# LSH attention followed by a gated convolution layer: part of the first batch's w_val products moved to earlier slots

## The chip, the cores and the metric

The kernel runs on one core of one Trainium2 chip. The metric is the device time of one execution in microseconds (us). The kernel before has a median of 624.18 us over three runs (622.38 to 624.53).

## The reference

Four batches of eight heads, 768 positions, head dimension 64, all in float32 (w_val, conv_w and w_out reach the kernel as float64). A hash gives each query and key a bucket of 6 bits, and a query sees only keys of its own bucket:

```
q_bits = (einsum('bhsd,dk->bhsk', q, proj) > 0)        # the same for k
mask   = q_bucket[:, :, :, None] == k_bucket[:, :, None, :]
scores = where(mask, scale * q @ k^T, -1e9)
attn   = softmax(scores);  x = (attn @ v) as (batch, 768, 512)

gate_pre = sum over k of conv_w[k] * xp[:, k:k+768, :]   # causal, 5 taps
out = (sigmoid(gate_pre) * (x @ w_val)) @ w_out
```

The products with w_val and w_out are made in three parts each (high times high, low times high, high times low), from operands that are split into a rounded high part and a remainder.

## The kernel before

The attention works on 32 units (batch, head) of six query tiles each: 192 slots, numbered k. In one turn of the main loop (L519 to L531 of the code below) stand, for different tiles, the row maximum (DVE, L272), two small DVE instructions, the normalisation (POOL, L305), the scores of tile k + 1 (PE, L266), the exponential of tile k (ACT, L290), six transposes of tile k - 3 (PE, L314) and the copy of the transposes of tile k - 4 out of PSUM (ACT, L323). In every odd slot two steps of the product with v are made (PE, L337, eight matmuls). The order on each of PE, ACT, DVE and POOL is the order in which the code issues the instructions; each engine takes its own instructions strictly in turn. DMAs stand on SP's queue.

Beside this the loop advances generators, one step at a time, and a step is where a generator yields:

- `weights`: loads a 512 KB block of float64 weight (L137), and turns it into a high and a low part on ACT (L91), DVE (L93 to L109) and POOL (L111, L113). Eight blocks, done by about slot 52.
- `ahead` (`early_bits`): hash bits of the batches 2 to 4 (units 16, 20, 24 and 28). For each it loads four tiles `hh` and four tiles `hl` (L221, 192 KB each), makes four small matmuls into the PSUM tile `m` for each half (L226), compares on DVE (L229) and stores (L231). Eight such halves, called "bit halves" below, in the slots 16, 20, 28, 32, 40, 44, 52 and 56.
- `convs` (`pair_x`): for two heads at a time (a pair; four pairs in a batch) splits x into `xh` and `xl` and adds up the convolution. The last step of a batch's fourth pair takes the sigmoid of the four gates (ACT, L372, with table loads) and starts the batch's `moe`. For the first batch this is slot 65.
- `moe`: for each half of the positions (o) and each block of 128 columns (j), `val` makes 12 matmuls of 384 columns (L399), in steps of four, and multiplies by the gate (DVE, L404); `outp` makes 12 matmuls of 512 columns (L424), in steps of four. One batch has eight `val` and six `outp`. In the two slots at the sigmoid three steps are made, else one per slot, and one in every second slot where `thin` holds (for the first batch slots 90 to 101). Before its last two `outp` a batch waits for the next batch's `moe` (`hold`).

All `val` and `outp` of the main loop, and all bits made before the first `moe`, use the single PSUM tile `m` (pool `ps_m`, one buffer): the next group can start only when the last one has been read.

Of the kernel before, what the change touches and what calls it, by code (L numbers as in the profile page):

```python
# [8 lines left out]
FP32 = mybir.dt.float32  # L9
FP32R = mybir.dt.float32r  # L10
AF = mybir.ActivationFunctionType
ALU = mybir.AluOpType
# [14 lines left out]
def kernel(  # L27
# [10 lines left out]
    nc = tc.nc  # L38
    B, H, _, S = qk.shape
    P = 128  # L40
    D = 64
    KB = S // P
    HS = S // 2
    NP = H // 2
# [306 lines left out]
    def pair_x(b, c, x, gs, xs_):  # L351
        for o in (0, HS):
            xh = xs.tile([P, HS], FP32R, name="xh")
            xl = xs.tile([P, HS], FP32R, name="xl")
            xs_[(c, o)] = (xh, xl)
            x0 = x[:, KW - 1 + o:KW - 1 + o + HS]
            nc.vector.tensor_copy(out=xh, in_=x0)  # L357
            nc.gpsimd.tensor_tensor(out=xl, in0=x0, in1=xh.bitcast(FP32), op=ALU.subtract)  # L358
        yield
        g = gp.tile([P, S], FP32, name="g")  # L360
        gs.append(g)
        for k in range(KW):
            yield
            w = cw_sb[:, c * KW + k:c * KW + k + 1]
            if k == 0:
                nc.gpsimd.tensor_scalar(out=g, in0=x[:, 0:S], scalar1=w, scalar2=1.0, op0=ALU.mult, op1=ALU.mult)  # L366
            else:
                nc.vector.scalar_tensor_tensor(out=g, in0=x[:, k:k + S], scalar=w, in1=g, op0=ALU.mult, op1=ALU.add)  # L368
        if c == NP - 1:
            yield  # L370
            for g in gs:
                nc.scalar.activation(out=g, in_=g, func=AF.Sigmoid)  # L372
            cur["gates"] = 2
            moes.append(moe(b, xs_, gs))

    def acc_tile():
        pools = accs
# [6 lines left out]
    def moe(b, xs_, g):  # L384
        hs = {}
        todo = []

        def later():
            while todo:
                todo.pop(0)()  # L390

        def val(o, j):
            acc = acc_tile()
            m = 0
            for wi, xi in ((0, 0), (1, 0), (0, 1)):
                if m:
                    yield
                for c in range(NP):
                    nc.tensor.matmul(out=acc[:, 0:HS], lhsT=wv[wi][:, c, j * P:(j + 1) * P],  # L399
                                     rhs=xs_[(c, o)][xi], start=(m == 0), stop=(m == 11))  # L400
                    m += 1
                later()
            ht = hp.tile([P, HS], FP32, name="ht", bufs=2)
            nc.vector.tensor_tensor(out=ht, in0=acc[:, 0:HS], in1=g[j][:, o:o + HS], op=ALU.mult)  # L404

            def split():
                hh = hp.tile([P, HS], FP32R, name="hh")
                nc.vector.tensor_copy(out=hh, in_=ht)  # L408
                hl = hp.tile([P, HS], FP32R, name="hl")
                nc.gpsimd.tensor_tensor(out=hl, in0=ht, in1=hh.bitcast(FP32), op=ALU.subtract)  # L410
                hs[(o, j)] = (hh, hl)
            todo.append(split)
            yield
# [43 lines left out]

    raws, stacks, vts, ss, nbs, ps, tps, sums, rcs, nms, gs, cur = {}, {}, {}, {}, {}, {}, {}, {}, {}, {}, {}, {}
    avs, convs, moes, early = [], [], [], {}
    accs = [(ps_m, "m")]  # L460

    def step(gens):

        while gens:
            try:
                return next(gens[0])
            except StopIteration:
                gens.pop(0)
# [7 lines left out]
    with tc.manual_schedule(engines=ENGINES):  # L476
# [13 lines left out]
        for k in range(N + LAG + 1):  # L490
            if 0 <= k - LAG - 1:
                keep_transposed(k - LAG - 1)
            pair = k % 2 == 0 and 0 <= k - 2 < N
            if k < N:
                maxima(k)
            if pair:
                row_sums(k - 2)
            if k < N:
                factors(k)
            if pair:  # L500
                recip(k - 2)
            if 0 <= k - 2 < N:
                normalise(k - 2)
            if k < N:
                shifts(k)
            if k + 1 < N:
                if tiles[k + 1][0] != tiles[k][0]:
                    finish(preps)
                    preps = [prep(tiles[k + 1][0] + 1)]
                scores(k + 1)  # L510
            if k < N:
                exponentials(k)
            if k >= 60 or k % 2:
                step(convs)
            for _ in range((1, 0, 2, 0, 2, 2)[k % 6]):
                step(weights[turn])
                turn = 1 - turn

            thin = k // 6 % 8 in (7, 0) and k < 186  # L519
            for _ in range(3 if cur["gates"] else (1, 0)[k % 2] if thin else 1):  # L520
                step(moes)
            cur["gates"] = max(0, cur["gates"] - 1)
            step(preps)
            if 6 <= k < 60 and k % 6 in (2, 4):
                step(ahead)
            if k % 2:
                step(avs)
                step(avs)
            if 0 <= k - LAG < N:
                transposes(k - LAG)  # L530
# [67 lines left out]
```

## Time and profile before

| | |
|---|---|
| median of three runs | 624.18 us (622.38 to 624.53) |
| profiled execution, first to last instruction | 620.8 us |
| its own time outside the span | not listed; the median lies 3.4 us above the span |
| PE busy (matmul) | 585.5 us, 94% |
| DVE, ACT, POOL busy | 437.6, 421.4, 395.6 us |
| matmuls with w_val (L399) | 384 |
| matmuls with w_out (L424) | 288 |

Slot k is told by the k-th exponential (L290): its start is taken as the slot's boundary. Slot 12 begins at 42.81 us, slot 40 at 120.54, slot 56 at 165.13, slot 60 at 175.41, slot 66 at 195.98 and slot 108 at 314.74. A busy PE counts the modelled length of overlapping matmuls, so it is not PE at its peak.

### The profile page before, as it was taken

To read this page: it belongs to the slowest core of one execution; us is meant where nothing else is said; L and a number is where in the kernel's file an instruction comes from. 1 tells how busy PE (TensorE), PEld (TensorE's weight loads), DVE (VectorE), ACT (ScalarE), POOL (GpSimd) and SP (SyncE) were. 2 spreads that over 40 slices of the span, in tenths; PEclk is the share of its full clock that TensorE was granted. 3 is DMA by queue.
4 is the path that set the end of the run, shared out by engine and by line. 5 is a ranking of instruction groups with operands and counts; after the bars stand their busy time and mean duration, and the time that the engine had idled before them with its cause. 6 is when DMAs were issued, how large, how long until landed. Compare 5 with 4: busy or idle time off the path is not lost.

```text
span 620.8 us, 10648 instructions
## 1 busy us (share of the span) xinstructions
PE 585.5 (94%) x3496; PEld 423.4 (68%) x3496; DVE 437.6 (70%) x1017; ACT 421.4 (68%) x881; POOL 395.6 (64%) x373
## 2 busy tenths in 40 slices
PE   5789898989999999999999999999999999999997
PEld 2655565555657777776767777777667877775895
DVE  5869798998975866668575867569665877665532
ACT  2777777778778666777787676777787766765400
POOL 3576868778766765578564777568764777544321
PEclk9799999999999999999999999999999999999999
DMA  6467666564532235243433234333422213200111
GB/s 227 123 197 199 200 167 208 157 175 118 133 83 68 70 79 142 72 108 82 122 82 107 61 80 126 84 115 82 108 70 78 67 42 91 69 18 1 51 52 51
DMA packets 29031, 64.64 MB, mean 104 GB/s; under 512 B 4937, under 2 KB 10057, under 8 KB 28977
## 3 DMA queue, kind: packets, MB, share of 16 engines
q1 hardware_dynamic: 28832, 63.93, 37.8%
q8 instruction: 28, 0.46, 0.3%
q14 instruction: 27, 0.21, 0.1%
q10 hardware_dynamic: 144, 0.03, 0.0%
HBM read 30.60 MB, written 7.86 MB: 62 GB/s over the span
## 4 chain that ended last, share of the span: by engine, by line
PE 66%; DVE 12%; ACT 12%; DMA 5%; issue 3%; POOL 2%; SPq 1%; ACTq 0%; POOLq 0%; DVEq 0%
PE av L337 17%; PE s L266 16%; PE tp L314 12%; PE m L424 8%; PE m L399 7%; ACT p L290 5%; DVE nm L272 4%; ACT pt L323 3%; ACT x L345 2%; DMA w<-in_w_val_dram 2%; DVE g L368 2%; PE tp L399 1%; PE tp L424 1%; PE s L424 1%; DMA bk<-bq 1%
## 5 line engine op out<-in xcount | busy, mean ns | idle before, releaser
L305 POOL TENSOR_SCALAR p<-p,ri 128x768 f32<-128x768 f32 x192 | 210.5, 1100 | 156.0 <-DVE nb L282 130.8
L272 DVE TENSOR_REDUCE nm<-s 128x1 f32<-128x768 f32 x192 | 182.5, 950 | 61.2 <-PE s L266 61.0
L290 ACT ACTIVATE p<-s,nb,gs 128x768 f32<-128x768 f32 x192 | 192.6, 1003 | 46.2 <-DVE nb L282 41.9
L323 ACT COPY pt<-tp 128x384 f32<-128x384 f32 x384 | 165.7, 485 | 75.3 <-PE tp L314 74.4
L314 PEld LDWEIGHTS tp<-ident,p 128*128 128x128 f32 x1152 | 130.3, 142 | 72.2 <-issue 43.6
L314 PE MATMUL tp<-ident,p 128*128 128x128 f32 x1152 | 164.4, 279 | 2.6 <-ACT pt L323 2.1
L337 PE MATMUL av<-pt,vt 128*64 128x384 f32 x768 | 144.9, 498 | 0.0
L266 PE MATMUL s<-ak,aq 76*128 76x384 f32 x384 | 118.1, 389 | 23.2 <-ACT p L290 19.7
L266 PE MATMUL s<-bk,bq 128*128 128x384 f32 x384 | 101.3, 345 | 0.4 <-DVE bq L252 0.4
L337 PEld LDWEIGHTS av<-pt,vt 128*64 128x64 f32 x768 | 47.0, 136 | 61.5 <-issue 61.4
L266 PEld LDWEIGHTS s<-ak,aq 76*128 76x128 f32 x384 | 59.2, 194 | 38.7 <-ACT p L290 34.6
L368 DVE SCALAR_TENSOR_TENSOR g<-x,cw_sb,g 128x768 f32<-128x768 f32 x64 | 79.4, 1241 | 2.2 <-POOL g L366 2.1
L266 PEld LDWEIGHTS s<-bk,bq 128*128 128x128 f32 x384 | 71.7, 194 | 0.8 <-issue 0.8
L173 POOL TENSOR_TENSOR bq<-r,aq 128x768 fp32r<-128x768 f32 x31 | 59.2, 1909 | 0.1
L410 POOL TENSOR_TENSOR hl<-ht,hh 128x384 fp32r<-128x384 f32 x32 | 32.3, 1009 | 39.5 <-DVE hh L408 39.5
L345 ACT COPY x<-av 64x384 f32<-64x384 f32 x64 | 30.4, 475 | 29.7 <-PE av L337 29.0
L282 DVE TENSOR_SCALAR nb<-nm,gs 128x1 f32<-128x1 f32 x192 | 40.4, 211 | 3.5
L399 PE MATMUL m<-xh,wv 128*128 128x384 f32 x200 | 42.7, 337 | 0.0
L358 POOL TENSOR_TENSOR xl<-x,xh 128x384 fp32r<-128x384 f32 x32 | 33.4, 1059 | 13.8 <-DVE xh L357 13.8
L290 ACT ACTIVATION_READ_ACCUMULATOR p<-s,nb,gs 128x1 f32 x192 | 39.0, 203 | 0.0
L404 DVE TENSOR_TENSOR ht<-m,g 128x384 f32<-128x384 f32 x25 | 13.9, 556 | 35.6 <-PE m L399 29.2
L424 PE MATMUL m<-wo,hh 128*128 128x512 f32 x144 | 38.1, 394 | 0.0
(86 smaller groups left out, 486.9 us busy)
## 6 DMA issues: line engine op xcount, KB each, us to landing
r<-in_qk_dram SPq DMA_DIRECT2D x32, 384.0 KB
vt<-in_v_dram SPq DMA_DIRECT2D x16, 384.0 KB
out_dram<-o SPq DMA_DIRECT2D x24, 256.0 KB
ak<-aq SPq DMA_DIRECT2D x31, 192.0 KB
bk<-aq SPq DMA_DIRECT2D x31, 192.0 KB
bk<-bq SPq DMA_DIRECT2D x31, 192.0 KB
bq<-aq SPq DMA_DIRECT2D x31, 192.0 KB
hh<-in_qk_dram SPq DMA_DIRECT2D x16, 192.0 KB
```

Of the source, the lines that this page charges most:

```text
L173: nc.gpsimd.tensor_tensor(out=bq, in0=r, in1=aq.bitcast(FP32), op=ALU.subtract)
L266: nc.tensor.matmul(out=s[:, hf, 0:HS], lhsT=lq[0:n, qs], rhs=rk[0:n, hf * HS:(hf + 1) * HS], start=n == M, stop=n == P)
L272: nc.vector.tensor_reduce(out=nm, in_=s[:, :, 0:HS], axis=AX.XY, op=ALU.max, negate=True)
L290: nc.scalar.activation(out=p, in_=s[:, :, 0:HS], func=AF.Exp, bias=nb, scale=gs.pop(k), accum_out=sm[:, k % 2, 0:1])
L305: nc.gpsimd.tensor_scalar(out=p, in0=p, scalar1=rcs.pop(k), scalar2=1.0, op0=ALU.mult, op1=ALU.mult)
L314: nc.tensor.transpose(out=tp[:, n * P:(n + 1) * P], in_=p[:, kb * P:(kb + 1) * P], identity=ident)
L323: nc.scalar.copy(out=pt[:, :, qo:qo + P], in_=tp[:, 0:HS].rearrange("p (a b) -> p a b", b=P))
L337: nc.tensor.matmul(out=av[s * D:(s + 1) * D, 0:HS], lhsT=vt[:, kb, hh * D:(hh + 1) * D], rhs=pt[kb // 3][:, kb % 3, :], start=(kb == 0), s ...
L345: nc.scalar.copy(out=x[hh * D:(hh + 1) * D, o:o + HS], in_=av[s * D:(s + 1) * D, 0:HS])
L368: nc.vector.scalar_tensor_tensor(out=g, in0=x[:, k:k + S], scalar=w, in1=g, op0=ALU.mult, op1=ALU.add)
L399: nc.tensor.matmul(out=acc[:, 0:HS], lhsT=wv[wi][:, c, j * P:(j + 1) * P], rhs=xs_[(c, o)][xi], start=(m == 0), stop=(m == 11))
L424: nc.tensor.matmul(out=acc, lhsT=hs[(o, j)][hi][:, tb * P:(tb + 1) * P], rhs=wo[wi][:, j, :], start=(m == 0), stop=(m == 11))
```

## The change

After the second pair of the first batch, a new generator `first_sums` is queued in `begun`. In the even slots 40 to 54 it makes, for one (o, j) each, the products of the pairs that are there: two pairs (six matmuls) for the first half of the positions, three pairs (nine matmuls) for the second. In the odd slot after it ACT copies the sum from PSUM to SBUF. Later `val` of the first batch makes only the products of the remaining pairs (six or three matmuls), adds the kept sum on DVE, and multiplies by the gate in a second DVE instruction. `thin` now holds in every slot below 108, so the first batch's `moe` makes one step in every second slot there (and three in each of the slots 65 and 66). The bits ahead are stepped in every even slot from 6 to 38, so that the eight bit halves stand in the slots 12, 14, 20, 22, 28, 30, 36 and 38.

```
+        if (b, c) == (0, 1):
+            begun.append(first_sums(xs_))
...
+    def products(acc, xs_, o, j, cs, after=None):
+
+        todo = [(wi, xi, c) for wi, xi in ((0, 0), (1, 0), (0, 1)) for c in cs]
+        for m, (wi, xi, c) in enumerate(todo):
+            if m and m % NP == 0:
+                yield
+            nc.tensor.matmul(out=acc[:, 0:HS], lhsT=wv[wi][:, c, j * P:(j + 1) * P], rhs=xs_[(c, o)][xi],
+                             start=(m == 0), stop=(m == len(todo) - 1))
+            if after and (m % NP == NP - 1 or m == len(todo) - 1):
+                after()
+
+    def first_sums(xs_):
+
+        for i, (o, j) in enumerate((o, j) for o in (0, HS) for j in range(NP)):
+            cs = (0, 1) if o == 0 else (0, 1, 2)
+            acc = ps_m.tile([P, 512], FP32, name="m")
+            for _ in products(acc, xs_, o, j, cs):
+                pass
+            yield
+            t = xs.tile([P, HS], FP32R, name=("xh", "xl")[i % 2]).bitcast(FP32)
+            nc.scalar.copy(out=t, in_=acc[:, 0:HS])
+            parts[(o, j)] = (t, cs)
+            yield
...
         def val(o, j):
             acc = acc_tile()
-            m = 0
-            for wi, xi in ((0, 0), (1, 0), (0, 1)):
-                if m:
-                    yield
-                for c in range(NP):
-                    nc.tensor.matmul(out=acc[:, 0:HS], lhsT=wv[wi][:, c, j * P:(j + 1) * P],
-                                     rhs=xs_[(c, o)][xi], start=(m == 0), stop=(m == 11))
-                    m += 1
-                later()
+            part, done = parts.pop((o, j), (None, ())) if b == 0 else (None, ())
+            yield from products(acc, xs_, o, j, [c for c in range(NP) if c not in done], later)
             ht = hp.tile([P, HS], FP32, name="ht", bufs=2)
-            nc.vector.tensor_tensor(out=ht, in0=acc[:, 0:HS], in1=g[j][:, o:o + HS], op=ALU.mult)
+            if part is None:
+                nc.vector.tensor_tensor(out=ht, in0=acc[:, 0:HS], in1=g[j][:, o:o + HS], op=ALU.mult)
+            else:
+                nc.vector.tensor_tensor(out=ht, in0=acc[:, 0:HS], in1=part, op=ALU.add)
+                nc.vector.tensor_tensor(out=ht, in0=ht, in1=g[j][:, o:o + HS], op=ALU.mult)
...
+            if 40 <= k < 60 and k % 2:
+                step(begun)
             if k >= 60 or k % 2:
                 step(convs)
...
             thin = k // 6 % 8 in (7, 0) and k < 186
+            thin = thin or k < 108
...
-            if 6 <= k < 60 and k % 6 in (2, 4):
+            if 6 <= k < 40 and k % 2 == 0:
                 step(ahead)
+            if 40 <= k < 60 and k % 2 == 0:
+                step(begun)
```

In the issue order, `m`, `s`, `tp` and `av` are PSUM tiles, `wv_120` and `wv_121` the high and low part of w_val, `w_875`, `w_994`, `w_900` and `w_1019` blocks of weight. On PE at slots 40 and 41, before:

```order
L226 MATMUL m<-hh,proj_sb 32x384 x4
L314 MATMUL tp<-ident,p 128x128 x6
L266 MATMUL s<-ak,aq 128x384 x2
L266 MATMUL s<-bk,bq 128x384 x2
L337 MATMUL av<-pt,vt 64x384 x4
```

and on PE at the same place now:

```order
L384 MATMUL m<-xh,wv_120 128x384 x2
L384 MATMUL m<-xh,wv_121 128x384 x2
L384 MATMUL m<-xl,wv_120 128x384 x2
L314 MATMUL tp<-ident,p 128x128 x6
L266 MATMUL s<-ak,aq 128x384 x2
L266 MATMUL s<-bk,bq 128x384 x2
L337 MATMUL av<-pt,vt 64x384 x4
```

The bit half has gone to an earlier slot, and six matmuls with w_val stand in its place (L384 is the new line of L399). On SP at slots 18 to 23, where the fourth block of w_val is loaded, before:

```order
L177 DMA bq<-aq 64x768
L148 DMA r<-in_qk_dram 128x768
L137 DMA w_875<-in_w_val_dram 128x1024
L231 DMA ud<-ht 128x384
L182 DMA ak<-u 12x768
L221 DMA hl<-in_qk_dram 128x384 x2
L137 DMA w_994<-in_w_out_dram 128x1024
```

and on SP at the same place now:

```order
L177 DMA bq<-aq 64x768
L148 DMA r<-in_qk_dram 128x768
L221 DMA hl<-in_qk_dram 128x384 x3
L137 DMA w_900<-in_w_val_dram 128x1024
L231 DMA ud<-ht 128x384
L182 DMA ak<-u 12x768
L231 DMA ud<-ht 128x384
L137 DMA w_1019<-in_w_out_dram 128x1024
```

Three loads of `hl` now stand ahead of the weight block. On PE at the first `outp` of the first batch, before (L424):

```order
L424 MATMUL m<-wo_122,hh 128x512 x4
L314 MATMUL tp<-ident,p 128x128 x6
L266 MATMUL s<-ak,aq 128x384 x2
L266 MATMUL s<-bk,bq 128x384 x2
L424 MATMUL m<-wo_123,hh 128x512 x4
```

and on PE at the same place now (L447):

```order
L447 MATMUL m<-wo_122,hh 128x512 x4
L314 MATMUL tp<-ident,p 128x128 x6
L266 MATMUL s<-ak,aq 128x384 x2
L266 MATMUL s<-bk,bq 128x384 x2
L337 MATMUL av<-pt,vt 64x384 x4
L314 MATMUL tp<-ident,p 128x128 x6
L266 MATMUL s<-ak,aq 128x384 x2
L266 MATMUL s<-bk,bq 128x384 x2
L447 MATMUL m<-wo_123,hh 128x512 x4
```

A step came in every slot and now comes in every second. From slot 108 to the end the order on PE, DVE and ACT is the same in both kernels.

## Rows read from the trace of the kernel before

**Rows 1.** The page, part 1: busy time of each engine, share of the span, instructions.

```profile
PE 585.5 (94%) x3496; PEld 423.4 (68%) x3496; DVE 437.6 (70%) x1017; ACT 421.4 (68%) x881; POOL 395.6 (64%) x373
```

**Rows 2.** Stretches: from:to, length; busy of PE, PEld, DVE, ACT, POOL; clock, DMA share, GB/s.

```profile
42.81:120.54 77.73, 71.14 (x459) 44.37 (x457) 68.48 (x157) 59.61 (x128) 59.03 (x55) 1.00 0.66 186
120.54:143.94 23.40, 20.55 (x134) 13.14 (x133) 22.31 (x49) 16.46 (x36) 19.82 (x17) 1.00 0.56 162
143.94:165.13 21.19, 19.19 (x122) 11.98 (x124) 19.01 (x40) 16.70 (x36) 16.07 (x16) 1.00 0.41 99
165.13:175.41 10.28, 9.42 (x64) 6.22 (x57) 7.31 (x20) 7.41 (x18) 8.35 (x10) 1.00 0.51 134
175.41:195.98 20.57, 20.09 (x131) 14.32 (x130) 14.28 (x33) 17.58 (x34) 12.20 (x12) 1.00 0.31 74
195.98:213.25 17.27, 16.36 (x101) 12.20 (x100) 14.12 (x32) 11.87 (x26) 13.14 (x13) 1.00 0.28 74
213.25:231.18 17.93, 17.86 (x110) 13.51 (x109) 12.16 (x31) 12.13 (x28) 12.97 (x13) 1.00 0.39 93
231.18:249.79 18.61, 18.61 (x110) 13.64 (x109) 11.48 (x28) 13.07 (x30) 10.86 (x12) 1.00 0.45 118
249.79:267.51 17.72, 17.65 (x110) 13.51 (x109) 11.04 (x28) 12.41 (x29) 10.42 (x11) 1.00 0.31 83
267.51:283.13 15.62, 15.30 (x98) 11.35 (x97) 12.72 (x30) 12.10 (x27) 11.52 (x12) 1.00 0.32 88
283.13:298.40 15.27, 14.34 (x90) 9.88 (x89) 10.89 (x29) 11.92 (x27) 12.12 (x12) 1.00 0.45 107
298.40:314.74 16.34, 16.10 (x98) 11.49 (x97) 11.41 (x28) 12.36 (x29) 11.20 (x11) 1.00 0.35 99
335.44:352.92 17.48, 17.40 (x110) 13.44 (x109) 12.70 (x32) 12.12 (x28) 12.02 (x12) 1.00 0.26 73
406.92:422.31 15.39, 15.31 (x98) 11.35 (x97) 11.66 (x30) 12.00 (x27) 10.91 (x12) 1.00 0.29 83
```

**Rows 3.** The same, of L290 alone: two instructions per slot.

```profile
42.81:120.54 77.73, 30.56 (x56) 1.00 0.66 186
```

**Rows 4.** Chain of waits, shares by line: 42.81 to 120.54, then 195.98 to 314.74.

```profile
by line: DVE nm L272 10.1%; DMA w<-in_w_val_dram 8.2%; issue 7.2%; DMA w<-in_w_out_dram 6.7%; DMA bk<-bq 6.5%; PE av L337 5.6%; PE s L266 5.6%; POOL bq L173 5.3%; DVE g L368 4.4%; DMA hl<-in_qk_dram 4.1%; ACT p L290 3.1%; DVE o L94 2.5%; DV
...
by line: PE av L337 24.3%; PE s L266 22.2%; PE tp L314 17.4%; PE m L424 9.4%; PE m L399 8.3%; ACT p L290 7.3%; ACT pt L323 5.3%; ACT x L345 2.6%; issue 1.9%; DVE nm L272 0.7%; DVE ht L404 0.5%; DVE nb L282 0.2%; DVE gs L278 0.1%; ACTq L290 
```

**Rows 5.** Chain of waits in the tail, where PE works without a gap: start, us, what.

```profile
577.41 2.75 PE tp L424 x12
...
582.91 2.10 PE tp L399 x12
```

**Rows 6.** DVE's waits, 42.81 to 120.54: us in total, times, longest.

```profile
DVE o L93 <- ACT o L91: 2.9, 2, 1.8
...
DVE ht L229 <- PE m L226: 1.7, 3, 1.1
```

**Rows 7.** Groups by shape: shapes, count, busy us, mean ns, idle before, releaser.

```profile
L323 ACT COPY pt<-tp 128x384 f32<-128x384 f32 x384 | 165.7, 485 | 75.3 <-PE tp L314 74.4
...
L404 DVE TENSOR_TENSOR ht<-m,g 128x384 f32<-128x384 f32 x25 | 13.9, 556 | 35.6 <-PE m L399 29.2 <-ACT g L372 3.4 <-issue 1.8
...
L229 DVE TENSOR_SCALAR ht<-m,packed 128x384 fp32r<-128x384 f32 x8 | 5.4, 676 | 4.3 <-PE m L226 4.2
```

**Rows 8.** Timeline of SP, 62 to 75 us: start, us, instruction.

```profile
66.55 0.44 SPq L137 DMA_DIRECT2D w<-in_w_val_dram  x1
...
70.98 0.98 SPq L221 DMA_DIRECT2D hl<-in_qk_dram  x2
```

**Rows 9.** Timeline of ACT: start, us, instruction, idle before it and its releaser.

```profile
72.96 0.70 ACT L91 ACTIVATE o<-w 128x512 f32<-128x512 f32 x1 [1.67 <-DMA w<-in_w_val_dram]
...
190.88 3.05 ACT L372 ACTIVATE g<-g 128x768 f32<-128x768 f32 x4
```

More of the change, by code (lines that the diff above doesn't have):

```diff
@@ L459 @@
     avs, convs, moes, early = [], [], [], {}
+    begun, parts = [], {}
     accs = [(ps_m, "m")]
```

## The prediction

> **What bounds the kernel now.** I read the page's first part, then the stretches, then the chain of waits of two of them. PE is busy for 94% of the span [rows 1], but the share is an average over two regimes, and the reader should see where they meet. From slot 66 the chain runs over PE: av, s, tp and the two products m take 82% of it, DVE about 1% (second line of [rows 4]). From slot 12 to 39 the chain mixes DVE (nm and the weights' conversion), loads of weights and POOL, and PE has no large share (first line of [rows 4]); DVE is busy for 68.48 of 77.73 us there, and for 22.31 of 23.40 us in slots 40 to 47 [rows 2]. So matmuls taken out of the slots from 66 on are worth time, and a DVE instruction put into the slots before 40 costs time.
>
> What a slot costs when PE alone sets it: the stretch at 335.44 us has six slots with one step of four 384-column matmuls each, and takes 17.48 us with PE busy for 17.40 [rows 2]. A matmul of 384 columns takes 2.10 / 12 = 0.175 us without a gap, one of 512 columns 2.75 / 12 = 0.229 us [rows 5]. That leaves (17.48 - 24 x 0.175) / 6 = 2.21 us of PE per slot for s, tp and av. The same from a thin stretch with three steps (406.92): (15.39 - 2.10) / 6 = 2.21.
>
> **The change, stretch by stretch.** The order from slot 108 on is the same, so the 306 us from 314.74 on stay. Up to slot 11 nothing moves. Between them are five terms.
>
> *Slots 12 to 39* (28 slots, by the 56 instructions of L290 [rows 3]). Four of the eight bit halves come in from slots 40 to 56: four DVE compares of 0.676 us, 2.7 us, and each waits for its own matmuls, 4.2 / 8 = 0.53 us on average [rows 7], 2.1 us more. DVE takes its instructions in turn, and behind each compare stands the next row maximum, on which exponential, scores and so the slot depend. That is 4.8 us if nothing covers it. Twice (slots 14 and 38) the bit half stands right behind bits of the next four units in the one PSUM buffer, and PE must wait for DVE to read; I count that inside the next item's spread. The loads move too: three hl loads now go out just ahead of a weight block on SP's queue. That block goes out at 66.55 us and ACT already waits 1.67 us for it, at 72.96 [rows 8, 9]. ACT takes its instructions in turn, so its exponentials stand behind this wait. Issue of three loads is 3 x 0.49 = 1.5 us [rows 8], and their 0.59 MB at the stretch's 186 GB/s [rows 2] another 3.2 us: at most 4.7 us. But the slots before have become later themselves by a bit half or two (1.2 us each), and the compares of slots 20 and 22 lie under the same wait, so I take 0.5 us net. Term: +5.3 us. Ends: 0 (DVE's 9.25 us of idle time in the stretch, of which 2.9 us is this kind of weight wait [rows 6], would hide all of it; a gain has no source, as instructions are only added) and 4.8 + 4.7 = +9.5.
>
> The Trainium skill (DMA: Bandwidth & Descriptors, section Queues, rings and completion order) says that on each DMA engine descriptors are consumed in ring order. By that rule the block waits for all of the three loads, and the upper end holds; the block took 6.4 us from issue to ACT's start here, which neither confirms nor excludes it. It is the second rival below.
>
> *Slots 40 to 55.* PE gets 4 x 6 + 4 x 9 = 60 matmuls, 60 x 0.175 = 10.5 us. The stretch takes 23.40 + 21.19 = 44.59 us now, set by DVE. Three bit halves leave it, and DVE's 41.32 us fall to 39.3. PE needs 16 x 2.21 + 10.5 = 45.9 us, so the bound passes from DVE to PE, and the stretch becomes longer, not shorter. With both engines over 80% busy the nearest row is the stretch at 195.98 us, where PE is busy for 16.36 of 17.27 us with DVE at 82%: some 2 to 5% of gaps. I take 47.0 us: +2.4 us. Ends: +1.3 (no gap) and +6.9 (nothing of the matmuls is hidden: 10.5 less three bit halves of 1.2). The eight ACT copies, 0.485 us each by the copy of the same shape from PSUM [rows 7], lie beside ACT's idle time (33.2 busy of 44.6 us) and each follows an exponential whose scores PE made just before the sum, so it finds it ready; the next sum wants the buffer a slot later. If that cover went, 8 x 0.485 = 3.9 us, within the upper end.
>
> *Slots 56 to 59.* One bit half leaves: 0.68 + 0.53 = 1.2 us at most. DVE has more idle time here (7.31 of 10.28 us busy), so I take -1.0; ends -1.2 and 0.
>
> *Slots 60 to 65, the sigmoid.* Slots 65 and 66 make 18 matmuls in place of 24, but the four sigmoids and two table loads hold ACT until slot 66 begins at 195.98 [rows 9], and PE's work lies beside that. The added DVE adds lie there too. Term 0; ends -1.0 and +1.7 (three adds of 0.556 us [rows 7] that are not hidden).
>
> *Slots 66 to 107.* The other 54 of the 60 matmuls leave: 9.4 us of PE. The steps now come in every second slot. I price each six slots from the thin row nearest to it [rows 2]: with three outp steps 16.34 (298.40), with three full val steps 15.39 (406.92), with little else 15.27 (283.13).
> - 66 to 71: 17.27 becomes 15.9. Only six matmuls stay, but DVE has 14.12 us and one add more, so not below 15.4.
> - 72 to 77, one short val and two outp steps: 17.93 becomes 15.9.
> - 78 to 83 and 84 to 89, three outp steps each: 18.61 and 17.72 become 16.34 each.
> - 90 to 95: 15.62 becomes 15.4; 96 to 101: 15.27 stays; 102 to 107: 16.34 stays, three outp steps before and after.
>
> Sum of after 111.5, of before 118.76: -7.3 us. Ends: -11.8 (PE alone: 42 x 2.21 + 18 x 0.175 + 48 x 0.229 = 107.0) and -3.9 (the first two stretches stay, as DVE's convolution for the next batch fills them). The eight second DVE instructions, about 0.56 us each, fall in stretches where DVE is busy for 11 to 14 of 16 us; in the first one that is what keeps 15.9.
>
> Sum: 5.3 + 2.4 - 1.0 + 0 - 7.3 = -0.6 us on the profiled execution's span of 620.8. The page lists no time of its own for what lies around the span; the median of the runs is 3.4 us above it, and I carry that over: 624.18 - 0.6 = 623.6 us. What slots 66 to 107 give back is spent before slot 56.
>
> **Rivals.**
> - *Clearly faster.* The early compares hide under DVE's and ACT's waits for weights, and PE's saving comes almost whole. For it: DVE idles 9.25 us before slot 40, and PE's chain from slot 66 is nearly pure. Against: the chain there passes DVE again and again, and thin stretches stay above PE's own 13.3 us plus products. 2.0 + 1.8 - 1.0 - 8.5 = -5.7: 618.5 us.
> - *Slower, by the weights' queue.* The three hl loads ahead of the block, and ACT standing in turn behind it, cost the whole 4.7 us and the compares do not lie under it: 9.5 + 2.4 - 1.0 - 7.3 = +3.6: 627.8 us. It decides when ACT's wait for this block passes about 5 us in place of 1.67. The ring-order rule named above speaks for it; that later blocks are used several slots after their issue speaks against it happening elsewhere.
> - *The change does not do what it says.* The freed PE time does not become shorter slots, as DVE and ACT hold the rhythm of the thin slots: -3.9 in place of -7.3, total +2.8: 627.0 us. For it: the stretch at 283.13 takes 15.27 us where PE alone would need 13.98. Against: two outp stretches with full steps go to 18.61, above any thin row.
>
> **How the numbers follow.** About 0.5% (3.1 us) is what a measurement of this kernel can tell from no change. Forecast 0.46, faster rival 0.25, weights' queue 0.19, no return 0.10. Forecast alone: 620.5 to 626.5. The range reaches to both outer rivals, 618.0 to 628.5. Faster by over 0.5% (below 621.1): the faster rival and a tail of the forecast, 0.27. Slower (above 627.3): most of the weights' queue and part of the last rival, 0.21. Within: 0.52.
>
> **What would show it.** Slot 108 should begin at about 314 us as now, slot 66 some 6 to 7 us later than 195.98, slot 40 some 5 us later than 120.54. In slots 40 to 55 the chain should have turned from DVE to PE and ACT's copies should wait for nothing. ACT's wait before the fourth block's L91 should stay below 4 us. From slot 66 to 107 no stretch should pass 16.5 us. I am wrong if slot 40 begins less than 2 or more than 9 us later, or if slots 40 to 55 do not become longer.

## The result, and the profile after

The changed kernel takes 630.71 us (median of six runs, 627.15 to 633.23), the kernel before 622.71 us in the runs beside it (621.29 to 624.53). The ratio is 1.0121, 95% interval 1.009 to 1.0153: slower by 8.0 us. The forecast was 623.6 us, its range 618.0 to 628.5.

The profiled execution took 631.42 us, its span is 629.6 us (before 620.8). First the page's part 1 of the changed kernel, which answers to [rows 1]:

```profile
PE 589.3 (94%) x3496; PEld 422.4 (67%) x3496; DVE 443.2 (70%) x1025; ACT 423.2 (67%) x889; POOL 398.2 (63%) x373
```

PE's 3496 instructions are as many as before. DVE and ACT have eight more each. Nothing here tells where 8 us went. The stretches do (from:to, length; busy time of PE, PEld, DVE, ACT, POOL; clock, DMA share, GB/s), cut at the slots of [rows 2]:

```profile
43.20:129.63 86.43, 77.92 (x491) 45.43 (x490) 70.54 (x161) 59.64 (x128) 59.17 (x55) 1.00 0.66 184
129.63:152.98 23.35, 22.04 (x138) 16.40 (x137) 22.37 (x47) 17.78 (x40) 20.93 (x17) 1.00 0.35 95
152.98:177.03 24.05, 23.90 (x151) 18.65 (x150) 17.37 (x40) 18.13 (x42) 17.48 (x17) 1.00 0.44 104
177.03:186.67 9.64, 8.98 (x56) 6.05 (x56) 6.58 (x19) 7.19 (x18) 6.83 (x9) 1.00 0.28 74
186.67:207.29 20.62, 18.84 (x119) 12.46 (x118) 16.20 (x36) 17.56 (x33) 11.72 (x11) 1.00 0.20 52
207.29:224.34 17.05, 15.77 (x95) 10.82 (x94) 14.34 (x34) 11.95 (x26) 12.90 (x13) 1.00 0.48 116
224.34:241.42 17.08, 15.82 (x95) 10.86 (x94) 13.35 (x31) 11.96 (x26) 14.01 (x13) 1.00 0.31 76
241.42:257.24 15.82, 15.82 (x98) 11.46 (x97) 11.38 (x28) 12.42 (x29) 10.41 (x11) 1.00 0.44 121
257.24:273.06 15.82, 15.82 (x98) 11.46 (x97) 10.78 (x27) 12.43 (x28) 10.66 (x11) 1.00 0.38 97
273.06:290.18 17.12, 16.39 (x100) 11.73 (x99) 13.46 (x33) 12.50 (x29) 12.01 (x12) 1.00 0.30 90
290.18:306.86 16.68, 14.08 (x85) 9.16 (x84) 13.34 (x31) 11.88 (x27) 14.00 (x13) 1.00 0.41 99
306.86:322.66 15.80, 15.80 (x98) 11.46 (x97) 11.19 (x28) 12.42 (x29) 10.41 (x11) 1.00 0.41 109
```

Slots 12 to 39 take 86.43 us in place of 77.73, and DVE is busy only 2.06 us longer: the rest is waiting. In the last seven lines (slots 66 to 107, 115.37 us in place of 118.76) PE is the bound, with no idle time, only in the three stretches of 15.8 us. In the four others it stands still for 0.7 to 2.6 us, and they are the slow ones.

| slots | before | after | difference | forecast |
|---|---|---|---|---|
| 12 to 39 | 77.73 | 86.43 | +8.70 | +5.3 |
| 40 to 55 | 44.59 | 47.40 | +2.81 | +2.4 |
| 56 to 59 | 10.28 | 9.64 | -0.64 | -1.0 |
| 60 to 65 | 20.57 | 20.62 | +0.05 | 0 |
| 66 to 107 | 118.76 | 115.37 | -3.39 | -7.3 |

With 0.39 us before slot 12 this makes slot 108 begin 7.92 us later, and the last exponential 7.86 us later. The remaining 1.0 us of the span lie behind it, in unchanged code. The last matmul ends as far behind the last exponential as before (54.5 us, before 54.6); the 1.0 us stand behind that matmul, at the last store, and the same is seen in one other kernel of this study (`e3_resident`).

**The early slots.** What DVE waited for from slot 12 to 39 (us in total, times, longest), to be held against [rows 6]:

```profile
DVE ht L229 <- PE m L226: 10.5, 6, 4.6
```

The compare's wait for its matmuls was 1.7 us in three cases and is 10.5 in six. What made the matmuls late stands in the waits of PE's weight loads, which go ahead of the matmuls, in the same stretch:

```profile
PEld m L226 <- DVE u L207: 3.6, 2, 1.9
...
PEld m L226 <- DMA hl<-in_qk_dram: 2.3, 3, 1.6
PEld m L226 <- DMA hh<-in_qk_dram: 1.4, 2, 1.0
```

Two causes, then: twice the buffer `m`, still to be read by the in-line compare (L207), and five times a load that has not landed. The chain of waits shows one of each (start, us, what). First slot 14, then slots 20 to 23:

```profile
48.62 1.28 DVE w L101
49.89 0.60 DVE u L207
50.49 0.04 issue
50.54 0.85 PE m L226 x8
...
68.35 5.50 DMA hl<-in_qk_dram
73.84 0.04 issue
73.89 1.87 PE m L226 x6
75.76 0.02 issue
75.78 0.68 DVE ht L229
76.46 0.88 DVE nm L272
```

At 50 us a weight conversion stands ahead of the compare that frees `m`, on DVE, which works in order. PE, which also works in order, holds back everything behind the bit half until then. Slot 14 takes 4.33 us in place of 2.68, slot 38 (the same pattern) 4.84 in place of 2.69: 3.8 us together. The half's own time is part of these 3.8 us; `e13_spaced` below tells the two apart. At 73.84 the last `hl` load lands, and the row maximum at 76.46 waits behind the compare of the half that needed it: slot 22 takes 5.87 us in place of 4.09. SP (start, us, instruction) and ACT at the same place, answering to [rows 8, 9]:

```profile
68.35 1.49 SPq L221 DMA_DIRECT2D hl<-in_qk_dram  x3
69.88 0.43 SPq L137 DMA_DIRECT2D w<-in_w_val_dram  x1
```

```profile
76.12 0.68 ACT L91 ACTIVATE o<-w 128x512 f32<-128x512 f32 x1 [3.03 <-DMA w<-in_w_val_dram]
```

From the block's issue to ACT's start are 6.24 us, with three loads just ahead of it; before it was 6.41 (66.55 to 72.96). ACT's wait grew by 1.36 us: slot 22 begins 1.80 us later than before, the block's issue 3.33.

**Slots 40 to 55.** The chain's shares by line, 129.63 to 177.03:

```profile
by line: PE av L337 18.3%; PE s L266 16.9%; PE m L384 15.4%; PE tp L314 15.4%; DVE nm L272 5.5%; ACT p L290 4.4%; ACT x L345 3.7%; ACT pt L323 3.6%; DVE g L370 3.1%; DVE w L101 2.7%; DVE w L97 2.6%; DVE o L94 2.2%; DVE nb L282 1.3%; issue 1
```

Four lines of PE hold 66% of it: the bound has passed from DVE to PE, as forecast.

**The late slots.** The chain over slots 92 to 95, at two short `val`:

```profile
278.56 0.54 PE m L384 x3
279.10 0.02 issue
279.12 0.57 DVE ht L426
279.69 0.02 issue
279.71 1.12 DVE ht L427
280.84 0.88 DVE nm L272
```

The chain leaves PE for DVE: after three matmuls of 0.54 us come the add (L426), the multiplication (L427), and only then the row maximum. Their durations in the whole kernel (ns, min/median/max):

```profile
L427 DVE TENSOR_TENSOR ht<-ht,g x8: 558/677/1266, 203.1 to 291.8; 128x384 f32<-128x384 f32 x8
```

```profile
L426 DVE TENSOR_TENSOR ht<-m,xh x4: 550/556/557, 200.8 to 284.9; 128x384 f32<-128x384 f32 x4
```

The eight multiplications take 6.27 us together, 0.784 us each, where the one they replace, with `m` in PSUM, took 0.556 [rows 7].

### The profile page after: what moved, and what is told of

Same layout as the page of the kernel before. It is cut to its first block, busy times and chain, and to the rows that moved or that the text cites. A ratio compares the mean times of both kernels' runs of the same rounds, so it can differ in the third digit from the quotient of the medians.

```text
span 629.6 us, 10676 instructions
## 1 busy us (share of the span) xinstructions
PE 589.3 (94%) x3496; PEld 422.4 (67%) x3496; DVE 443.2 (70%) x1025; ACT 423.2 (67%) x889; POOL 398.2 (63%) x373
## 3 DMA queue, kind: packets, MB, share of 16 engines
HBM read 30.60 MB, written 7.86 MB: 61 GB/s over the span
## 4 chain that ended last, share of the span: by engine, by line
PE 66%; DVE 15%; ACT 9%; DMA 5%; issue 2%; POOL 1%; SPq 0%; ACTq 0%; DVEq 0%; POOLq 0%
PE av L337 16%; PE s L266 15%; PE tp L314 12%; PE m L447 8%; PE m L384 7%; ACT p L290 5%; DVE nm L272 4%; ACT pt L323 3%; DVE g L370 2%; ACT x L345 2%; PE tp L384 1%; PE tp L447 1%; PE s L447 1%; DMA bk<-bq 1%; POOL bq L173 1%
## 5 line engine op out<-in xcount | busy, mean ns | idle before, releaser
L290 ACT ACTIVATE p<-s,nb,gs 128x768 f32<-128x768 f32 x192 | 192.4, 1002 | 55.7 <-DVE nb L282 53.0
L370 DVE SCALAR_TENSOR_TENSOR g<-x,cw_sb,g 128x768 f32<-128x768 f32 x64 | 81.4, 1272 | 2.2 <-POOL g L368 2.1
L173 POOL TENSOR_TENSOR bq<-r,aq 128x768 fp32r<-128x768 f32 x31 | 59.5, 1919 | 0.1
L384 PE MATMUL m<-xh,wv 128*128 128x384 f32 x200 | 43.2, 338 | 1.3 <-DVE ht L426 1.3
L290 ACT ACTIVATION_READ_ACCUMULATOR p<-s,nb,gs 128x1 f32 x192 | 39.0, 203 | 0.0
L447 PE MATMUL m<-wo,hh 128*128 128x512 f32 x144 | 38.1, 394 | 0.0
L384 PEld LDWEIGHTS m<-xh,wv 128*128 128x128 f32 x200 | 35.3, 188 | 2.2 <-DVE ht L426 1.9
```

What stands on the lines that cost most here:

```text
L173: nc.gpsimd.tensor_tensor(out=bq, in0=r, in1=aq.bitcast(FP32), op=ALU.subtract)
L290: nc.scalar.activation(out=p, in_=s[:, :, 0:HS], func=AF.Exp, bias=nb, scale=gs.pop(k), accum_out=sm[:, k % 2, 0:1])
L447: nc.tensor.matmul(out=acc, lhsT=hs[(o, j)][hi][:, tb * P:(tb + 1) * P], rhs=wo[wi][:, j, :], start=(m == 0), stop=(m == 11))
```

## The experiments

All times of stretches below are cut at L290 like those above. The changed kernel's code of slots 12 to 39 is also in four of the experiments. In all five it took 85.0 to 86.4 us, median 85.45, so one profile tells differences there to about 0.7 us.

| | 12 to 39 | 40 to 55 | 56 to 65 | 66 to 107 | ratio to before (95%) |
|---|---|---|---|---|---|
| before | 77.73 | 44.59 | 30.85 | 118.76 | |
| after | 86.43 | 47.40 | 30.26 | 115.37 | 1.0121 (1.009 to 1.0153) |
| `e1_bits_only` | 85.03 | 44.48 | 30.25 | 118.70 | 1.0081 (1.0064 to 1.0099) |
| `e2_sums_only` | 77.92 | 52.34 | 31.04 | 114.78 | 1.0077 (1.0053 to 1.0101) |
| `e3_resident` | 83.10 | 47.37 | 30.26 | 114.75 | 1.0082 (1.0057 to 1.0106) |
| `e5_loads_early` | 85.33 | 47.45 | 30.30 | 115.45 | 1.0181 (1.0156 to 1.0206) |
| `e4_no_add` | 85.45 | 47.45 | 33.34 | 112.57 | 1.0077 (1.0054 to 1.01) |
| `e8_no_compare` | 82.11 | 47.40 | 30.26 | 116.96 | 1.0043 (1.0012 to 1.0074) |
| `e11_no_ahead` | 75.90 | 47.34 | 30.26 | 117.84 | 1.0069 (1.0044 to 1.0094) |
| `e12_ident` | 85.90 | 47.41 | 32.38 | 114.42 | 1.012 (1.0092 to 1.0148) |
| `e13_spaced` | 81.71 | 47.38 | 30.29 | 115.48 | 1.0047 (1.0026 to 1.0068) |
| `e14_fused` | 85.29 | 47.43 | 30.27 | 120.36 | 1.0175 (1.0152 to 1.0198) |
| `e15_both` | 81.85 | 47.33 | 30.27 | 120.33 | 1.0131 (1.0108 to 1.0154) |
| `e16_fewer` | 81.30 | 45.79 | 30.79 | 114.95 | 0.9983 (0.9971 to 0.9996) |

### The bits' half of the change alone

`e1_bits_only`, against the kernel before:

```
-            if 6 <= k < 60 and k % 6 in (2, 4):
+            if 6 <= k < 40 and k % 2 == 0:
```

> The kernel before with one part of the change alone: the bits of the batches ahead stepped in every even slot from 6 to 38. Nothing else. If the loss before slot 40 belongs to the bits (theory), slots 12 to 39 take 86.4 us as in the changed kernel, against 77.7 before; slots 40 to 55, which lose three bit halves and stay bound by DVE, fall from 44.6 to about 41; slots 56 to 107 as before; in all about +4 to +5 us. Rival (the loss before slot 40 comes from something else in the changed kernel): slots 12 to 39 stay near 78.

The whole early loss is here (85.03). A surprise is that slots 40 to 55 gain nothing, though three bit halves leave them and about 41 us were expected. A part of the chain there:

```profile
140.77 1.04 POOL wo L113
...
141.83 5.71 DMA w<-in_w_out_dram
```

The load of the last weight block, whose buffer POOL frees late, holds the chain for 5.71 us, and ACT waits 1.29 us for it, where it did not wait before. Slots 40, 44 and 52, which lose a half each, are 2.4 us shorter together, but slot 46, where that wait lies, is 1.4 us longer (3.69 in place of 2.28), and slots 41 and 53 take the rest.

### The sums' half alone

`e2_sums_only`, against the changed kernel:

```
-            if 6 <= k < 40 and k % 2 == 0:
+            if (6 <= k < 40 and k % 6 in (2, 4)) or (40 <= k < 60 and k % 6 in (3, 5)):
                 step(ahead)
```

> The changed kernel with the bits of the batches ahead at their old places as far as they fit: up to slot 38 as before, the last two sets one slot later, in odd slots (halves in 41, 45, 53 and 57). Theory: slots 12 to 39 return to 77.7 us; slots 40 to 55 take 47.4 us as in the changed kernel if the halves hide beside the matmuls, up to 51 if each adds 1.2; slots 66 to 107 stay at 115.4. In all between -1 and +3 us against before. Rival (the sums and the bits block each other in the single buffer): slots 40 to 55 over 52 us and the whole slower than +4.

Without the early halves, slots 12 to 39 are back at 77.92. But bits and sums then share `m` in slots 40 to 55, which take 52.34 us, as the rival said. What PE waited for in 121.29 to 173.63:

```profile
PE m L226 <- ACT xh L398: 4.3, 3, 1.8
```

A bit half waits for ACT's copy of the sum just ahead of it in `m`: 1.4 us on average. So the loss is the bits', and the two halves of the change need each other.

### Bit halves that wait for no load

`e3_resident`:

```
+    still = const.tile([P, HS], FP32, name="still")
+    nc.gpsimd.memset(still, 1.0)
...
-                    nc.tensor.matmul(out=z[32 * jj:32 * jj + 32, 0:HS], lhsT=proj_sb, rhs=t, start=True, stop=True,
+                    nc.tensor.matmul(out=z[32 * jj:32 * jj + 32, 0:HS], lhsT=proj_sb, rhs=still, start=True, stop=True,
```

> The changed kernel, but the matmuls of the bits ahead read a tile that is always there in place of the loaded ones (the loads are still made, their data is not used, so the bits of the batches 2 to 4 are not the hash bits). It takes away the wait for the loads and nothing else. Theory of the load waits (PE stands in turn at these matmuls until hh or hl has landed, and DVE behind it): slots 12 to 39 fall from 86.4 to 81 to 83.5 us. Rival (the halves' own DVE time, and the weight block behind the hl loads): they stay at 85 or more.

83.10: waiting for loads is 2.35 us of the median 85.45, not the whole. Slots 14 and 38 stay at 4.25 and 4.74 us, so the collisions in `m` owe next to nothing to the loads. Slot 28 falls most (3.18 us, from 4.84). Slot 22 hardly falls (5.57 us): the half there no longer waits, but ACT waits 3.17 us for the weight block behind the loads, and the chain now goes over the block's load:

```profile
67.15 6.09 DMA w<-in_w_val_dram
```

### The loads one step earlier

`e5_loads_early`, in `early_bits` (core of the edit):

```
+        rows = [load(16, 0)]
+        yield
+        rows.append(load(16, 1))
+        yield
         for i in range(16, len(units), 4):
...
                 nc.sync.dma_start(out=u[:, hf * HS:(hf + 1) * HS], in_=t)
+                if i + 4 < len(units):
+                    rows[hf] = load(i + 4, hf)
```

> The changed kernel with the loads for the bits ahead issued earlier (each half of the next set right behind the matmuls that free its tiles, eight slots ahead of their use in place of four); matmuls and compares in the same slots as in the changed kernel. Theory of the load waits: slots 12 to 39 fall from 86.4 to 82 to 84 us, the whole to about +4 to +5 us against before. Rival (the halves' own DVE time and the weight block): they stay at 85 or more, as the same loads still stand ahead of the weight blocks.

A miss: the first loads now go ahead of an earlier weight block, and ACT waits 5.04 us for that one. Slots 6 to 11 take 18.74 us in place of 15.22, and slots 12 and 13 another 1.6 us more. Slots 22 and 28, where loads were waited for, do fall (to 3.25 and 3.26 us), but 12 to 39 as a whole stay at 85.33. The slowest kernel of all: the wait only moves along SP's queue.

### No compares, no matmuls for the bits ahead

`e8_no_compare`:

```
-                z = ps_m.tile([P, 512], FP32, name="m")
...
-                nc.vector.tensor_scalar(out=t.bitcast(FP32R), in0=z[:, 0:HS], scalar1=rows_sb[:, 0:1],
-                                        scalar2=rows_sb[:, 1:2], op0=ALU.is_ge, op1=ALU.mult)
+                t = rows[hf][0]
```

> The changed kernel with the loads of hh and hl and the stores kept, but the matmuls and DVE compares of the bits ahead left out (a loaded tile is stored as it is, so the bits of the batches 2 to 4 are wrong). Theory (each of the eight halves costs about 1.2 us on the way of DVE, beside the load waits): slots 12 to 39 fall from 86.4 to 72 to 76 us. Rival (the halves are covered; the loads and the weight blocks behind them cost the time): they stay at 79 or more.

82.11 is far above the 72 to 76 expected, and above the 79 that the rival named. Slots 14 and 38 are back at 2.69 and 2.73, but slot 22 takes 6.74. Slots 22 to 24 of this kernel, one line each:

```profile
68.28:75.02 6.74, 3.44 (x21) 1.92 (x20) 1.89 (x5) 2.39 (x6) 4.38 (x5) 0.94 0.88 284
75.02:76.83 1.81, 1.81 (x8) 1.65 (x9) 1.76 (x7) 1.81 (x6) 0.07 (x1) 0.50 0.76 196
76.83:79.57 2.74, 2.74 (x13) 2.64 (x12) 1.79 (x4) 1.94 (x6) 2.74 (x2) 0.50 0.28 90
```

ACT waits 4.4 us for the weight block here, though no matmul and no compare of the bits is left: the loads ahead of the block hold slot 22 by themselves, as the rival said. PE stands still meanwhile and then works at half of the full clock. Slots 22 to 25 take 15.64 us against 13.31 in the changed kernel. The 2.3 us between them are a price of the longer wait and of the slow clock behind it, so this run doesn't tell what a half costs; taken off, about 79.8 would remain. The clock fell once more in slots 98 and 99 (0.74 and 0.73), which is why slots 66 to 107 take 116.96 us here.

### No bits ahead

`e11_no_ahead`:

```
-        ahead = [early_bits()]
+        ahead = []
```

> The changed kernel without any bits ahead: the bits of units 16, 20, 24 and 28 are made in line at their turn, from tiles that are there anyway, in the slots from about 85 on. Theory (the halves cost 1.2 us each before slot 40, the waits for their loads another 3): slots 12 to 39 take 72 to 75 us, 40 to 107 as in the changed kernel but for one set, and the four sets cost together 4 to 8 us later; the whole between -3 and +3 us against before. Rival (the early loss is not theirs): slots 12 to 39 stay above 80 and the whole is slower than the changed kernel.

75.90, a little above the 72 to 75 expected, so eight halves with their loads and waits cost 9.5 us there, and before's four 1.8. The in-line sets come later instead: slots 84 to 89 take 17.99 us and slots 108 to 159 take 159.88 in place of 155.20. The whole is 3.7 us slower than before, where at most 3 were expected: to leave the bits out early is no gain.

### The halves kept clear of the in-line bits

`e13_spaced`:

```
-            if 6 <= k < 40 and k % 2 == 0:
+            if k in (6, 8, 9, 12, 13, 14, 16, 20, 22, 23, 24, 29, 30, 31, 32, 36, 37):
                 step(ahead)
```

> The changed kernel with the same eight bit halves before slot 40, but in other slots: 12, 13, 20, 22, 29, 30, 36 and 37, so that none shares a slot with the bits made in line (slots 14, 15, 38, 39), and with loads that no longer stand just ahead of the fourth weight block and lead their use by four to seven slots. Theory (the early loss is collisions in the one PSUM buffer, waits for loads, and the weight block behind the loads): slots 12 to 39 fall from about 86 to 79 to 81.5 us, the whole to between 0 and +3 us against before. Rival (the halves' own time on DVE, about 1.2 us each): slots 12 to 39 stay at 83 or more.

Slots 14 and 38 fall to 2.67 and 2.72, slot 22 to 3.65, and the stretch to 81.71, 0.2 us above the range expected. This run takes away more than the collisions. No matmul of the bits waits for a load here, and the compare's wait for its matmuls is less than half of the changed kernel's 10.5 us:

```profile
DVE ht L229 <- PE m L226: 4.5, 6, 2.0
```

So the gain has to be read by place. Slots 12 to 15 and 36 to 39 hold two halves each in both kernels, and only their order to the in-line bits differs. They take 12.03 and 11.74 us in place of 13.19 and 12.99, 2.4 us less (2.1 less than in `e3_resident`, where no half waits for a load). That is the price of the two collisions; the rest of the 3.8 us of slots 14 and 38 is the halves' own time, which now stands in the slots beside them. Slots 22, 23 and 28 to 31, where the changed kernel waits for loads and for the weight block, give another 2.4 us. What is left above before, 4.0 us, is 1.0 us on average for each of the four extra halves, without collisions and without waits for loads.

### No add

`e4_no_add`:

```
-            if part is None:
+            if True:
                 nc.vector.tensor_tensor(out=ht, in0=acc[:, 0:HS], in1=g[j][:, o:o + HS], op=ALU.mult)
```

> The changed kernel, but val of the first batch leaves the kept sum out (it is made and copied, and not added, so the first batch's output lacks it): one DVE instruction per val in place of two; all other engines keep their order. Theory (the second DVE instruction of each val, in slots where DVE also carries the next pair's convolution, sets those slots): slots 66 to 107 fall from 115.4 to 110 to 112 us, nearly all of it in 90 to 101, where 33.8 become about 31. Rival (the rhythm of a step in every second slot sets them): 66 to 107 stay at 114.5 or more.

Slots 66 to 107 give 2.8 us more (112.57, just above the 110 to 112 expected): slots 90 to 95 fall from 17.12 to 15.67, slots 66 to 71 from 17.05 to 16.16. DVE's second instruction holds 2.8 of the 3.9 us that were missing from the forecast gain. In slots 66 to 71 it is less the instruction than its length: `e2_sums_only` and `e3_resident` have the add and the same code there and take 16.4 us, because there the multiplication of slot 70 took 0.56 and 0.57 us, and 1.27 in the changed kernel. Against these two the add is worth 2.2 us. But the stretch of the sigmoid loses 3.1 us. There PE waited:

```profile
PE m L384 <- DVE ht L424: 3.6, 2, 2.9
```

The add of the changed kernel reads `m` early, ahead of the sigmoid; the multiplication must wait for the gate and keeps `m`.

### The kept sum added on PE

`e12_ident` (core of the edit):

```
+            if part is not None:
+                nc.tensor.matmul(out=acc[:, 0:HS], lhsT=ident, rhs=part, start=True, stop=False)
```

> The changed kernel with the kept sum added on PE: one float32 matmul of the identity by the kept tile opens each val of the first batch, and DVE's second instruction goes. Theory (DVE's adds): slots 90 to 101 fall from 33.8 to 31.5 us or less; slots 66 to 107 take 111 to 113.5, as PE pays 0.36 to 0.8 us for each of five such matmuls. Rival (rhythm): 66 to 107 stay at 115 or rise.

114.42, between theory and rival, and 2.1 us more at the sigmoid, for the same reason: no gain in all. Slots 90 to 95 stay at 17.10: the added matmul takes 0.65 us on PE, so one wait is exchanged for another, and the run does not decide between the two.

### The gate's product on POOL as well

`e14_fused`, and `e15_both` with the steps of `e13_spaced` too:

```
-                nc.vector.tensor_tensor(out=ht, in0=ht, in1=g[j][:, o:o + HS], op=ALU.mult)
...
+                    nc.vector.tensor_tensor(out=hh, in0=ht, in1=gj, op=ALU.mult)
+                    nc.gpsimd.tensor_tensor(out=ht, in0=ht, in1=gj, op=ALU.mult)
```

> The changed kernel with DVE's third instruction of each val of the first batch taken away, the result kept right: DVE adds the kept sum, then multiplies by the gate straight into the rounded high part (no cast), and POOL makes the product again for the remainder. Theory (DVE's added instruction is what slots 66 to 107 lack): 66 to 107 fall from 115.4 to 112 to 113.5 us, slots 60 to 65 stay at 20.6, as the buffer m is still freed before the sigmoid. Rival (POOL, with 12 to 14 of 16 us busy, takes DVE's place): 66 to 107 stay at 115 or rise.

> The spacing of the bits and the fused split together. If both theories hold the two gains add: slots 12 to 39 at 79 to 81.5 us, 40 to 55 at 47.4, 66 to 107 at 112 to 113.5; the whole between -3 and +2 us against before, so about level with it or slightly faster. Rival: the gains do not add, because the bound passes to another engine, and the whole stays slower than before by more than 3 us.

Slots 66 to 71 of `e14_fused`:

```profile
204.98:223.87 18.89, 16.72 (x102) 11.57 (x100) 14.76 (x32) 11.99 (x27) 17.46 (x18) 1.00 0.33 88
```

POOL, busy for 17.46 of 18.89 us, has become the bound (three of its lines hold 35% of the chain there): 120.36 in place of 115.37, as the rival said. `e15_both` shows that the two edits act apart: 81.85 early and 120.33 late.

### Fewer sums, fewer early halves

`e16_fewer`:

```
-        for i, (o, j) in enumerate((o, j) for o in (0, HS) for j in range(NP)):
+        for i, (o, j) in enumerate([(0, 0), (0, 1), (0, 2), (0, 3), (HS, 0), (HS, 1)]):
...
-            thin = thin or k < 108
+            thin = k < 98 or thin and k >= 108
...
-            if 6 <= k < 40 and k % 2 == 0:
+            if k in (6, 8, 9, 12, 13, 14, 16, 20, 22, 23, 24, 29, 30, 36, 38, 52, 56):
                 step(ahead)
```

> Six kept sums in place of eight (the last two of the second half of the positions are made whole later), six bit halves before slot 40, spaced so that none stands right behind the in-line bits, and the last two in slots 52 and 56 again; the first batch's moe steps every second slot up to 97 and every slot from 98 to 107. Theory (the early slots pay for each bit half put there, about 1 to 2 us even without a collision; the late slots return only PE's time less DVE's second instruction): 12 to 39 takes 78.5 to 80.5 us (before 77.73, spaced eight halves 81.71), 40 to 55 takes 44.5 to 46 (42 matmuls in place of 60, one half back), 56 to 59 as before, 66 to 107 takes 116.5 to 118 (18 matmuls, 3.2 us, come back, two adds leave); sum about +1 us on before, 622 to 625, ratio 0.999 to 1.004. Rival (only the halves' crowding costs anything, and six sums keep most of the gain): 12 to 39 at 77.7 to 78.5 and 66 to 107 at 115 to 116, 618 to 621, ratio below 0.997.

621.97 us against 622.98, a ratio of 0.9983 (0.9971 to 0.9996): the only kernel that beats the one before, by 1.0 us. It gains late more than theory and rival said, 114.95: without the last two kept sums, and with a step in every slot from 98 on, the stretch is no longer than with them. The two edits are not told apart here, but the last two sums are not needed for the gain. It loses early more than expected (81.30 against 78.5 to 80.5), in slot 37, where the clock falls again (slots 36 and 37):

```profile
110.51:112.41 1.90, 0.77 (x3) 0.77 (x4) 1.74 (x4) 1.83 (x4) 1.90 (x2) 0.83 0.90 281
112.41:117.42 5.01, 5.01 (x25) 2.49 (x27) 3.64 (x7) 2.78 (x6) 5.01 (x6) 0.73 0.61 173
```

PE stood still for 1.30 us in slot 36, and the eight matmuls of av behind it took 2.49 us in place of 1.51. Slot 37 takes 3.30 us in `e13_spaced`, which has a bit half there; with that the stretch would be 79.6, inside the range expected.

## Why the prediction was wrong

**Slots 12 to 39, the first step that failed.** The forecast counted the two bit halves behind in-line bits in `m` "inside the next item's spread", at nothing. These collisions cost 2.1 to 2.4 us, by `e13_spaced`. The price is not the compare's 0.676 us but the reader's whole queue: what stands ahead of it on DVE, then the matmuls on PE, then the second compare. The loads are the other part that was too small: 0.5 us net, with the compares of slots 20 and 22 under ACT's wait for the weight block. The waits for loads alone are 2.35 us (`e3_resident`), and loads and block together 2.4 us in `e13_spaced`. The halves' own time was sized about right, 4.0 us against 4.8.

**The weights' queue.** This rival's total came nearest of the three, and its mechanism is there, but not at its price. ACT's wait became 3.03 us, under its point of about 5, and slot 22 grew by 1.78 us. In the changed kernel the chain of slot 22 goes over `hl`, but the block comes close to it: ACT, held up by the block, waits only 0.31 us more for the chain's row maximum. Without the wait for `hl`, slot 22 keeps 5.57 of its 5.87 us (`e3_resident`), and with nothing left but the loads it takes 6.74, at an ACT wait of 4.4 us (`e8_no_compare`). With the loads at other places it takes 3.65 us, at a wait of 1.23 (`e13_spaced`); in `e5_loads_early`, where they go ahead of an earlier block, ACT waits 5.04 us for that one. The block itself took no longer from issue to use than before (6.24 us against 6.41; 5.11 in `e13_spaced`): it went out later. The Trainium skill (DMA: Bandwidth & Descriptors, section Queues, rings and completion order) has descriptors consumed in ring order. The order of landing agrees with it (`hl` at 73.84 us, the block used at 76.12); the upper end that it would have borne out is not in this trace.

**Slots 40 to 59 and the sigmoid.** Right in mechanism and size: 47.40 against 47.0, with PE busy for 45.94 of it, ACT's copies without a wait, and the adds hidden beside the sigmoid. `e4_no_add` shows that the adds even help there: they free `m`. Only the credit for the three bit halves that leave has no support: without the sums the stretch does not become shorter (`e1_bits_only`). It did not matter, as PE became the bound.

**Slots 66 to 107, the second step that failed.** The forecast let the second DVE instruction cost something in the first stretch alone. By stretch, measured less forecast: +1.15, +1.18, -0.52, -0.52, +1.72, +1.41, -0.54, in sum +3.9. The stretches of pure `outp` came out better than the thin rows they were priced by. All four with `val` came out worse, and without the add (`e4_no_add`) 2.2 to 2.8 us of it go. The next batch's convolution is no mark of the four: it stands on DVE in the stretches of pure `outp` too. Idle time of DVE in the stretch was no cover: three short matmuls are done in 0.54 us, and then add and multiplication both stand between PE's work and the next row maximum. The instruction was also mis-sized, 0.784 us in place of 0.556. The 1.1 us that `e4_no_add` leaves, in slots 72 to 77 and 96 to 101, stand beside another DVE instruction that became longer: the convolution's step L370 of slots 72 and 96 takes 2.23 us in both, beside POOL's L173, where the same step took 1.61 and 1.01 before. It lies on the chain, here in slot 96:

```profile
293.68 2.15 DVE g L370
```

In `e4_no_add` the two take 2.56 and 2.58 us, so leaving out the add does not give this back. The size fits, but no run separates it. The rival "no return" had this nearly right (-3.9 against -3.4 measured); what it lacked was that the early loss would grow at the same time.

**By the signs named beforehand.** Slot 108 begins at 322.66 us and not at 314, slot 66 11.3 us later and not 6 to 7, slot 40 9.1 us later, beyond the 9 named, and four late stretches pass 16.5 us. The chain on PE in slots 40 to 55, ACT's wait below 4 us and the unchanged time from slot 108 to the last exponential came as said.

## What to carry to other kernels

Before moving work into a single-buffered tile on engines that work in order, list in the new order what stands just ahead of each use: a use right behind another costs the reader's queue, here 1.0 to 1.25 us more than the same use one slot earlier. Where two waits end close together, as at slot 22, taking away the later one gives back only what lies between them. Price time that is freed on the bounding engine by the chain that is left, with every added instruction on it; where the freed work was also the cover of another engine, less comes back. A gap on PE is paid twice if the clock falls behind it, so look at the granted clock before reading a stretch of an experiment as saving or loss.

## What the runs showed of the hardware that was not expected

**The clock after a gap.** From slot 6 to the last exponential the granted clock is 1.00 in every stretch of six slots, before and after. In `e8_no_compare` PE stood still for 3.07 us and was granted 0.50 in the next two slots, the lower of its two levels (1.2 GHz), and six transposes took 1.51 us in place of 0.82:

```profile
68.37 0.82 PE L308 MATMUL tp<-ident,p 128*128 128x128 f32 x6
...
74.90 1.51 PE L308 MATMUL tp<-ident,p 128*128 128x128 f32 x6 [3.07 <-ACT pt L317]
```

The same stands behind slot 37 of `e16_fewer` (0.73) and part of the loss at the sigmoid in `e4_no_add` (0.93 over that stretch).

**Two operands in SBUF beside POOL.** The multiplication L427 took 0.56 to 0.62 us in four cases, 0.73 and 0.78 in two, and 1.12 and 1.27 in two. At 279.71 us POOL was at work, as it was at a step of the convolution (L370) that took long; DVE, then POOL (start, us, instruction):

```profile
279.71 1.12 DVE L427 TENSOR_TENSOR ht<-ht,g 128x384 f32<-128x384 f32 x1
...
293.59 2.23 DVE L370 SCALAR_TENSOR_TENSOR g<-x,cw_sb,g 128x768 f32<-128x768 f32 x1
```

```profile
278.41 2.01 POOL L358 TENSOR_TENSOR xl<-x,xh 128x384 fp32r<-128x384 f32 x2 [0.30 <-DVE xh L357]
...
293.20 1.82 POOL L173 TENSOR_TENSOR bq<-r,aq 128x768 fp32r<-128x768 f32 x1
```

The convolution's step L370 takes 1.01 us alone and 2.23 beside POOL's L173: 295.02, where POOL ends, and 1.01 more would be 296.03, and it ended at 295.82. All 30 steps of L370 in the changed kernel that took over 1.1 us ended 0.80 to 0.82 us after a POOL instruction that had run beside them. The add, which reads one operand from PSUM, stayed at 0.55 to 0.56 in all eight cases. The Trainium skill (SBUF — State Buffer, section SBUF: two separate sides) says that a DVE instruction with two SBUF inputs and a POOL instruction that reads SBUF exclude each other for the whole instruction; the trace agrees to about 0.2 us.
